# W_out issued second, w1 - w2 in quarters, w2 cast by GpSimd, and three first-stage matmuls in place of spins

## The chip, the cores and the metric

The kernel runs on one core of a Trainium2 chip. A core has TensorE (matrix products, into PSUM), VectorE (DVE in the profile), ScalarE (ACT), GpSimd (POOL) and SyncE (SP); each works through its own instructions in order, and waits on semaphores for the others. DMAs are issued from SyncE (the hardware queue, q1 in the profile) and from GpSimd (the software queue, q0, which also converts f32 to bf16 on the way). The metric is the device time of one execution in microseconds (us). Lower is better.

## The reference

The input x has 8 batches of 3072 rows and 256 columns, f32. Each column is filtered in the frequency domain, and the result goes through a gate of two weight matrices and an output matrix:

```python
X = np.fft.rfft(x, axis=1)
Y = X * (filt_r + 1j * filt_i)[None]
y = np.fft.irfft(Y, n=3072, axis=1).reshape(8 * 3072, 256)
h1, h2 = y @ w1, y @ w2                 # w1, w2: 256 x 1024
out = np.maximum(h1, h2) @ w_out        # w_out: 1024 x 256
```

## The kernel before

The gate is rewritten as max(h1, h2) = max(y (w1 - w2), 0) + h2. So out = relu(y Wd) W_out + y M, with Wd = w1 - w2 and M = w2 W_out, both made once on the chip. Wd comes from GpSimd (`prep_wd`, two halves of 512 columns). For M, VectorE casts w2 to bf16 (`cast_w2`, four casts of 512 columns), TensorE transposes it (`prep_t`, two halves), and 16 products with W_out follow (`prep_m`).

The Fourier transform of 3072 points is done in two stages of 96 and 32 as matmuls. For one batch: the first stage (`f1` for batch 1, `s1` for batches 2 to 7) over chunks of x; its result goes to a DRAM buffer `ad` and is read back in another layout as `bt`; the second stage (`s2`), the product with the filter on VectorE, and the inverse of the second stage (`s3`) follow; the result goes through a DRAM buffer `zd` and comes back as `zr`; the inverse of the first stage (`s4`) gives a tile `y` of 384 rows, transposed. Batch 0 avoids the DRAM buffers: it uses transposes on TensorE (`t1`, `t2`). For batches 2 to 7, x is loaded as f32 by SyncE (`load_xf`, eight chunks in three rotating buffers XF), and GpSimd adds and subtracts the two halves of the batch (`fold`, one add and one subtract a chunk); chunk c of `s1` needs fold c, and the load of chunk c + 3 needs fold c to have freed its buffer. For batches 0 and 1, x is loaded and cast by GpSimd's queue (`load_x`).

The main loop goes over 64 tiles `tt` of 384 rows plus one round to finish. Each tile has 8 steps. In a step, `moe_h` makes one block of 128 hidden units (two products with Wd, then a relu on ScalarE or VectorE into `gt`), and `moe_o` makes three or four of the 30 products of the tile before it (for each of three blocks c of 128 rows: eight with W_out and two with M, summed in PSUM tile `po`). Two neighbouring sums share a `po` tile, which VectorE copies to `ot`, and GpSimd's queue writes it to the output. Everything else hangs in this loop by step numbers: `plan(b, step, fn)` puts a function into step `step` of batch b's 64 steps, and all engines meet their instructions in this written order. `plan_f1` gives the steps of `f1` for batch 1 and of the read of `ad` (`f1_read`). `plan_f2` gives the visits of the next batch's second stage; in its first call they stand at steps 24, 28, 31, 35, 38, 42 and 46 of batch 0's 64, work on batch 1, and carry the `s1` chunks of batch 2 with them (chunk 0 at step 24, chunk 1 at step 28, chunk 2 at step 31). Its two last lists are the steps of `load_xf` and of `fold`.

Before the loop lies a setup: tables of sines, batch 0's first and second stage, the filter's products, and the loads of the weights. `spin` makes matmuls whose result nobody reads, while TensorE waits. At the end of the setup stand GpSimd's last loads of batch 1, the two halves of Wd, the load of W_out (`load_wo`), and the table CT that `s1` reads; then the first `f1`, `t2` and `s4`. Step 0 of the loop begins at about 37.5 us.

Tiles in the profile: Wo is W_out, WS holds w1 and w2 in f32, w2b and w2T are w2 cast and transposed, ph is a hidden block in PSUM, pa a first-stage result, px a second-stage result, pd a spin, xb is x in bf16.

Of the kernel before, what the change touches and what calls it, by code (L numbers as in the profile page):

```python
# [8 lines left out]
FP32 = mybir.dt.float32  # L9
# [6 lines left out]
D = 256  # L16
# [10 lines left out]
def kernel(  # L27
# [15 lines left out]
    V, S, G, TE = nc.vector, nc.scalar, nc.gpsimd, nc.tensor  # L43
# [15 lines left out]
    w2b = const.tile([128, 2, HID], BF16)  # L59
# [9 lines left out]
    pso = ctx.enter_context(tc.tile_pool(name="pso", bufs=2, space=bass.MemoryType.PSUM))  # L69
# [8 lines left out]
    def x_tile(b, c):  # L78
        if c % 2 == 0:
            xb[b] = xpool.tile([128, 8, D], BF16, tag="xb", name="xb")  # L80
        return xb[b][:, 4 * (c % 2):4 * (c % 2) + 4]

    def load_x(b, c, n):
        for k in range(c, c + n):
            xb[b, k] = x_tile(b, k)[0:NP]
        src = x[b].rearrange("(p m) d -> p m d", m=NM)
        m0 = 4 * (c % 2)
        G.dma_start(out=xb[b][0:NP, m0:m0 + 4 * n], in_=src[:, 4 * c:4 * c + 4 * n, :])  # L88
# [98 lines left out]
    def table_ct():  # L187
        G.memset(CT, 0.0)
        for g in range(2):
            G.tensor_copy(CT[64 * g:64 * g + 48, :, 0:48].rearrange("p s (u r) -> p s u r", r=2),  # L190
                          C1[0:48].rearrange("p (u s r) -> p s u r", s=2, r=2))
# [85 lines left out]
    w1f, w2f = WS[:, 0:2], WS[:, 2:4]  # L277
# [3 lines left out]
        nc.sync.dma_start(out=w1f[:, :, js], in_=moe_w1.rearrange("(c p) j -> p c j", p=128)[:, :, js])  # L281
        nc.sync.dma_start(out=w2f[:, :, js], in_=moe_w2.rearrange("(c p) j -> p c j", p=128)[:, :, js])

    def cast_w2(h, c):
        V.tensor_copy(w2b[:, c, 512 * h:512 * h + 512], w2f[:, c, 512 * h:512 * h + 512])

    def load_wo():
        G.dma_start(out=Wo, in_=moe_w_out.rearrange("(c p) j -> p c j", p=128))

    def prep_wd(h, engine):  # L290
        js = slice(512 * h, 512 * h + 512)
        engine.tensor_tensor(Wd[:, :, js], w1f[:, :, js], w2f[:, :, js], OP.subtract)  # L292

    def prep_t(jp):
# [22 lines left out]
    def f1(b, c, engine):  # L317
        if c == 0:
            ad[b] = dram.tile([96, NM, D], BF16, tag="ad", name="ad")
        if c % 4 == 0:  # L320
            at_[b] = apool.tile([128, 8, D], BF16, tag="at", name="at")
        at = at_[b]
        pa = ps.tile([96, 2, D], FP32, tag="ps", name="pa")
        TE.matmul(pa, C1, xb[b, c // 2][:, 2 * (c % 2):2 * (c % 2) + 2], start=True, stop=True)
        o_ = at[0:96, 2 * (c % 4):2 * (c % 4) + 2]
        if engine is V:
            V.tensor_copy(o_, pa)
        else:
            S.activation(o_, pa, AF.Copy)
        if c % 2 == 1:  # L330
            m0 = 2 * (c % 4) - 2
            nc.sync.dma_start(out=ad[b][:, 2 * c - 2:2 * c + 2], in_=at[0:96, m0:m0 + 4])
# [121 lines left out]
    po = {}  # L454
    ot = {}

    def out_block(tt, c):
        b, i = divmod(tt, 8)
        dst = out[b * N:(b + 1) * N].rearrange("(c p i m) d -> c i p (m d)", c=3, p=32, i=8)[c, i]
        E = G if tt < 8 * B - 2 else nc.sync  # L460
        E.dma_start(out=dst, in_=ot[tt // 2][:, 3 * (tt % 2) + c])  # L461

    def moe_o(tt, k0, k1):
        y_, g_ = yt[tt], gt[tt]
        for k in range(k0, k1):
            c, e = divmod(k, 10)
            n = (e + 2) % 10 if tt == 0 else e
            q = 3 * tt + c
            blk = slice(128 * c, 128 * c + 128)
            if e == 0 and (q % 2 == 0 or q == 24 * B - 1):  # L470
                po[0] = pso.tile([128, 2, D], FP32, tag="po", name="po")
            p_ = po[0][:, q % 2]
            if n < 2:
                TE.matmul(p_, y_[:, n, blk], M[:, n], start=(e == 0), stop=(e == 9))  # L474
            else:
                TE.matmul(p_, g_[:, n - 2, blk], Wo[:, n - 2], start=(e == 0), stop=(e == 9))  # L476
            if e == 9 and q >= 24 * B - 2:
                e = q % 6
                if q % 2 == 0:
                    S.activation(ot[tt // 2][:, e], p_, AF.Copy)  # L480
                else:
                    V.tensor_copy(ot[tt // 2][:, e], p_)
                out_block(tt, c)
            elif e == 9 and q % 2 == 1:
                if q % 6 == 1:
                    ot[tt // 2] = opool.tile([128, 6, D], FP32, tag="ot", name="ot")
                e = q % 6
                V.tensor_copy(ot[tt // 2][:, e - 1:e + 1], po[0])  # L488
                for qq in (q - 1, q):
                    out_block(qq // 3, qq % 3)  # L490

# [26 lines left out]
    def s3t(v, pq):  # L518
        pool, tag = (ps, "ps") if v % 2 else (pso, "po")
        pz = [pool.tile([128, 2, 2, 2, 2, NM], FP32, tag=tag, name="pt%d" % g) for g in range(2)]  # L520
        for _ in range(2 if v == 1 else 1):
            TE.matmul(pz[0].rearrange("p i s r c m -> p (i s r c m)"), W1[:, 0:128], W1, start=True, stop=True)
        for i in range(2):
            for s in range(2):
                for dc in range(2):
                    for q, tab in enumerate((VP, VQ)):
                        for g in range(2):
                            TE.matmul(pz[g][:, i, s, :, dc], pq[s][64 * g:64 * g + 64, q, i, 128 * dc:128 * dc + 128],  # L528
                                      tab[64 * g:64 * g + 64, 2 * v + i, s].rearrange("p (r m) -> p r m", r=2),
                                      start=(q == 0), stop=(q == 1))  # L530
        zv = zT.rearrange("p c m (w g) q -> p w g (c m) q", g=2)
        for g in range(2):
            o_ = zv[:, 2 * v:2 * v + 2, g]
            i_ = pz[g].rearrange("p i s r c m -> p i (c m) (s r)")
            if v >= 4 and g == 1:
                V.tensor_copy(o_, i_)
            else:
                S.activation(o_, i_, AF.Copy)

    def t2(c, engines):  # L540
        if c == 0:
            zr[0] = zrpool.tile([96, NM, D], BF16, tag="zr", name="zr")
        n = 4 // len(engines)
        for k, engine in enumerate(engines):
            pr = ps.tile([96, n, D], BF16, tag="ps", name="pr")
            m0 = 4 * c + n * k
            for m in range(n):
                for dc in range(2):
                    TE.transpose(pr[:, m, 128 * dc:128 * dc + 128], zT[:, dc, m0 + m].rearrange("p u q -> p (u q)"),  # L549
                                 I128)  # L550
            if engine is V:
                V.tensor_copy(zr[0][:, m0:m0 + n], pr)  # L552
            else:
                S.activation(zr[0][:, m0:m0 + n], pr, AF.Copy)

    def spin(n):
        for _ in range(n):
            pd = ps.tile([128, 512], FP32, tag="ps", name="pd")
            TE.matmul(pd, W1[:, 0:128], W1, start=True, stop=True)  # L559
# [70 lines left out]
        pqs[v] = products(v)  # L630
    for v in (4, 5):
        s3t(v, pqs[v])
    for c in (2, 4):
        load_x(1, c, 2)
    prep_wd(0, G)
    load_wo()
    load_x(1, 6, 2)
    prep_wd(1, G)
    table_ct()
    setup.close()  # L640
    apool = ctx.enter_context(tc.tile_pool(name="apool", bufs=3))
# [4 lines left out]
    f1(1, 0, S)  # L646
    spin(1)
    t2(0, (V, S))
    spin(2)
    s4(0)  # L650
    spin(2)


    todo = {}
# [1 line left out]
    def plan(b, step, fn, *a):  # L656
        todo.setdefault((b + step // 64, step % 64), []).append((fn, a))

    def plan_f1(b, nb, steps, read):
        for c, n in zip(range(1, 16), steps):  # L660
            plan(b, n, f1, nb, c, S if c % 2 == 0 else V)
        plan(b, read, f1_read, nb)

# [11 lines left out]
            plan(b, steps[-1] + (6 if b else 11), s1_read, b + 2)  # L675

    plan(0, 2, t2, 1, (V,))
    for h in range(2):
        for c in range(2):
            plan(0, 3 + 2 * h + c, cast_w2, h, c)  # L680
    plan(0, 5, prep_t, 0)
    plan(0, 7, prep_t, 1)
    plan(0, 8, prep_m)
    for c in range(2, 8):
        plan(0, 8 * (c - 2) + 8, t2, c, (V,))
    plan_f1(0, 1, (0, 1, 1, 3, 4, 4, 5, 6, 6, 7, 8, 10, 11, 11, 12), 13)
    plan_f2(0, (24, 28, 31, 35, 38, 42, 46), ((0,), (1,), (2,), (3,), (4,), (5,), (6, 7)),
            (6, 10, 14, 18, 21, 25, 29, 33), (14, 18, 21, 25, 28, 32, 36, 40))
    for b in range(1, B - 1):
        plan_f2(b, (7, 14, 18, 24, 31, 38, 42) if b > 1 else (14, 18, 24, 30, 34, 39, 42), ((0, 1), (2,), (3,), (4,), (5,), (6,), (7,)),  # L690
                range(-32, 32, 8) if b > 1 else range(-25, 31, 7), range(-22, 42, 8) if b > 1 else range(-15, 41, 7))
# [1 line left out]
    for tt in range(8 * B + 1):  # L693
        b, i = divmod(tt, 8)
        k = 0
        for j in range(8):
# [5 lines left out]
            if tt > 0:  # L702
                n = 3 if j in (3, 7) else 4
# [36 lines left out]
```

## Time and profile before

| what | value |
| --- | --- |
| runs | 504.0, 504.1 and 504.84 us, median 504.1 |
| profiled execution | 503.8 us, its span 502.0 us |
| TensorE busy | 488.4 us, 97% of the span |
| VectorE, ScalarE, GpSimd busy | 331.9, 308.3, 257.5 us |
| granted clock of TensorE, mean | 0.992 |
| W_out's load: issue, landing | 37.19, 9.4 us later |
| loads of batch 1's chunks 2 and 3, 4 and 5, 6 and 7: landing after issue | 5.3, 6.6 and 10.9 us, issued at 33.8, 34.4 and 38.1 |
| w1 - w2 on GpSimd | 2 x 2.36 us, at 34.90 and 38.65 |
| read of batch 1 (bt from ad) | two DMAs of 768 KB, issued from 56.88, landing 5.8 and 8.4 us after issue |

The span begins with the first instruction; all times of rows count from there. A row of the timeline has the start, the duration, the engine, the line, the operation, output and inputs, the shape, the count and, in brackets, the idle time of that engine just before it with the instruction or DMA that ended it (inferred: where that one had long been done, it was another). TensorE's rows overlap, as matmuls are pipelined: the time that a matmul takes from others is the distance of starts (0.109 us for one of 256 columns, 0.163 for 384, 0.217 for 512). Rows of SyncE (SPq) are the issue of DMAs. A row of the DMA queues has packets, MB, and the time that the packets took as a share of the 16 DMA engines.

### The profile page before, as it was taken

The page shows a single profiled execution, that of the slowest core. Times are in us where ns is not written, and L with a number is a line of the kernel's source. Part 1 is how long each engine was busy: PE and PEld are TensorE (multiplying, and loading weights), DVE is VectorE, ACT ScalarE, POOL GpSimd, SP SyncE. Part 2 cuts the span into 40 slices and gives each one's busy share as a digit, 9 for nine tenths or more (in the row PEclk, how much of TensorE's full clock was granted, in tenths as well). Part 3 has the DMA queues.
Part 4 walks back from the last instruction along what each step waited for, and adds up shares of the span by engine and source line. Part 5 has one row for each costly group of instructions (what it writes and reads, how often), then busy time and mean ns, then how long its engine had stood idle before and what let it go on. Part 6 is the DMA issues. An engine that isn't in the chain of part 4 may idle for free.

```text
span 502.0 us, 13079 instructions
## 1 busy us (share of the span) xinstructions
PE 488.4 (97%) x5299; PEld 362.1 (72%) x5303; DVE 331.9 (66%) x518; ACT 308.3 (61%) x629; POOL 257.5 (51%) x338
## 2 busy tenths in 40 slices
PE   8688999999999999999999999999999999999997
PEld 3455777777777777777777777777777777777775
DVE  7876688457865777457765687557765687555553
ACT  6776478647774676557764586647774465544442
POOL 7893569547463864645654855537632221222220
PEclk9989999999999999999999999999999999999999
DMA  7999789995799667986779558896769235411112
GB/s 125 150 252 217 230 229 290 306 274 171 212 268 260 175 204 234 250 229 189 198 244 275 187 177 245 235 239 197 197 181 255 78 111 153 168 65 64 64 64 84
DMA packets 77966, 97.20 MB, mean 194 GB/s; under 512 B 8017, under 2 KB 54354, under 8 KB 77842
## 3 DMA queue, kind: packets, MB, share of 16 engines
q1 hardware_dynamic: 64642, 66.73, 49.6%
q0 software_dynamic: 13264, 29.64, 20.3%
q8 instruction: 41, 0.67, 0.6%
q14 instruction: 19, 0.16, 0.1%
HBM read 53.87 MB, written 47.19 MB: 201 GB/s over the span
## 4 chain that ended last, share of the span: by engine, by line
PE 90%; DMA 5%; POOL 2%; issue 1%; ACT 1%; DVE 0%; SPq 0%; POOLq 0%; DVEq 0%
PE po L476 34%; PE ph L448 33%; PE po L474 8%; PE pz L399 5%; PE py L428 4%; PE pa L349 2%; DMA F<-in_filt_r_dram 2%; PE px L376 2%; DMA Wo<-in_moe_w_out_dram 2%; POOL xb L88 1%; DMA F<-F 1%; PE pr L549 1%; POOL pq L382 0%; PE pt L528 0%; PE pm__1132 L306 0%
## 5 line engine op out<-in xcount | busy, mean ns | idle before, releaser
L476 PE MATMUL po<-Wo,gt 128*128 128x256 bf16 x1536 | 261.0, 273 | 0.2 <-DMA Wo<-in_moe_w_out_dram 0.2
L452 ACT ACTIVATE gt<-ph 128x384 bf16<-128x384 f32 x321 | 157.0, 496 | 147.9 <-PE ph L448 147.3
L461 POOL DMA_DIRECT2D out_dram<-ot x186 | 102.6, 555 | 187.1 <-DVE ot L488 184.4
L476 PEld LDWEIGHTS <-gt 128*128 128x128 bf16 x1536 | 146.6, 98 | 66.1 <-issue 10.3
L450 DVE TENSOR_SCALAR gt<-ph 128x384 bf16<-128x384 f32 x191 | 104.9, 552 | 63.1 <-PE ph L448 59.9
L382 DVE TENSOR_TENSOR pq<-px,F 128x1024 bf16<-128x1024 f32 x91 | 107.0, 1219 | 24.2 <-PE px L376 22.6
L448 PEld LDWEIGHTS <-Wd 128*128 128x128 bf16 x1024 | 96.5, 98 | 12.9 <-POOL Wd L292 1.4
L103 POOL TENSOR_TENSOR xb<-XF 128x512 bf16<-128x512 f32 x48 | 61.2, 1276 | 41.3 <-DMA XF<-in_x_dram 21.2
L488 DVE COPY ot<-po 128x512 f32<-128x512 f32 x95 | 65.1, 685 | 25.3 <-PE po L476 25.0
L104 POOL TENSOR_TENSOR xb<-XF 128x512 bf16<-128x512 f32 x48 | 61.0, 1271 | 0.0
L403 ACT ACTIVATE zt<-pz 128x512 bf16<-128x512 f32 x84 | 45.6, 595 | 11.5 <-PE pz L399 8.4
L353 ACT ACTIVATE at<-pa 128x512 bf16<-128x512 f32 x96 | 51.8, 610 | 1.2 <-PE pa L349 0.8
L428 PE MATMUL py<-G,zr 96*128 96x96 bf16 x512 | 32.7, 206 | 0.2
L428 PEld LDWEIGHTS <-zr 96*128 96x128 bf16 x512 | 29.0, 97 | 2.5 <-DVE zr L552 0.4
L399 PE MATMUL pz<-pq,VP 64*64 64x256 bf16 x336 | 21.9, 281 | 0.0
L376 PE MATMUL px<-bt,U 64*64 64x256 bf16 x384 | 19.8, 278 | 1.2 <-ACT VQ L273 0.7
L399 PE MATMUL pz<-pq,VQ 64*64 64x256 bf16 x336 | 20.9, 269 | 0.0
L349 PE MATMUL pa<-xb,CT 64*64 64x512 bf16 x192 | 19.5, 383 | 0.0
L399 PEld LDWEIGHTS <-VP 64*64 64x64 bf16 x336 | 9.7, 105 | 13.3 <-issue 13.3
L376 PEld LDWEIGHTS <-U 64*64 64x64 bf16 x384 | 10.4, 109 | 3.9 <-issue 3.3
L559 PE MATMUL pd<-W 128*128 128x512 bf16 x30 | 10.5, 462 | 1.7 <-DVE zero L145 1.5
L552 DVE COPY zr<-pr 96x1024 bf16<-96x1024 bf16 (+1 forms) x8 | 5.2, 649 | 8.0 <-PE pr L549 8.0
(429 smaller groups left out, 609.7 us busy)
## 6 DMA issues: line engine op xcount, KB each, us to landing
out_dram<-ot POOLq DMA_DIRECT2D x186, 128.0 KB, 3.3
XF<-in_x_dram SPq DMA_DIRECT2D x96, 192.0 KB, 4.6
ad<-at SPq DMA_DIRECT2D x56, 192.0 KB, 3.3
bt<-ad SPq DMA_DIRECT2D x14, 768.0 KB, 9.1
zd<-zt SPq DMA_DIRECT2D x42, 256.0 KB, 2.7
zr<-zd SPq DMA_DIRECT2D x56, 192.0 KB, 4.8
WS<-in_moe_w_dram SPq DMA_DIRECT2D x4, 512.0 KB, 5.1
xb<-in_x_dram POOLq DMA_DIRECT2D x8, 192.0 KB, 5.8
```

The lines of the kernel that those rows point to most:

```text
L103: G.tensor_tensor(t_[:, 0], f[:, 0], f[:, 1], OP.add)
L104: G.tensor_tensor(t_[:, 1], f[:, 0], f[:, 1], OP.subtract)
L353: S.activation(at[:, m0:m0 + 2], pa[g], AF.Copy)
L382: E.tensor_tensor(pq, px.rearrange("p (o i) d -> p o i d", o=1).to_broadcast([128, 2, 2, D]), F[:, :, 2 * v:2 * v + 2, s], OP.mult)
L399: TE.matmul(pz[g][64 * s:64 * s + 64, i], tab[64 * g:64 * g + 64, 2 * v + i, s], pq[s][64 * g:64 * g + 64, q, i], start=(q == 0), stop=(q ...
L428: TE.matmul(py[:, m], zr[b][:, 4 * i + m, 128 * dc:128 * dc + 128], G1, start=True, stop=True)
L448: TE.matmul(ph, Wd[:, dc, 128 * j:128 * j + 128], y_[:, dc], start=(dc == 0), stop=(dc == 1))
L450: V.tensor_scalar(gt[tt][:, j], ph, 0.0, None, OP.max)
L452: S.activation(gt[tt][:, j], ph, AF.Relu)
L461: E.dma_start(out=dst, in_=ot[tt // 2][:, 3 * (tt % 2) + c])
L476: TE.matmul(p_, g_[:, n - 2, blk], Wo[:, n - 2], start=(e == 0), stop=(e == 9))
L488: V.tensor_copy(ot[tt // 2][:, e - 1:e + 1], po[0])
```

## The change

Four things are edited. W_out's load becomes the second of GpSimd's steps after the filter's products, behind one load of x; the two other loads of x go behind three quarters of w1 - w2. w1 - w2 is made in four parts of 256 columns. The cast of w2 goes from VectorE to GpSimd, in two parts, behind the last quarter. Three `f1` of batch 1 (c = 1, 2, 3) come before the loop, and three spins go. The step lists follow: the transposes of w2 stand at steps 7 and 8 (before 5 and 7), M at step 10 (before 8), the other `f1` at new steps, and the loads and folds of batch 2 at later steps (the read of `ad` stays at step 13, the visits where they were). The first tile's 30 output products come in a new order, `FIRST`: blocks 0 and 2 with W_out, then their four products with M, then block 1; two `po` tiles are open at once.

```diff
--- before.py
+++ after.py
@@ -281,14 +281,14 @@
         nc.sync.dma_start(out=w1f[:, :, js], in_=moe_w1.rearrange("(c p) j -> p c j", p=128)[:, :, js])
         nc.sync.dma_start(out=w2f[:, :, js], in_=moe_w2.rearrange("(c p) j -> p c j", p=128)[:, :, js])
 
-    def cast_w2(h, c):
-        V.tensor_copy(w2b[:, c, 512 * h:512 * h + 512], w2f[:, c, 512 * h:512 * h + 512])
+    def cast_w2(h):
+        G.tensor_copy(w2b[:, :, 512 * h:512 * h + 512], w2f[:, :, 512 * h:512 * h + 512])
 
     def load_wo():
         G.dma_start(out=Wo, in_=moe_w_out.rearrange("(c p) j -> p c j", p=128))
 
-    def prep_wd(h, engine):
-        js = slice(512 * h, 512 * h + 512)
+    def prep_wd(q, engine):
+        js = slice(256 * q, 256 * q + 256)
         engine.tensor_tensor(Wd[:, :, js], w1f[:, :, js], w2f[:, :, js], OP.subtract)
 
     def prep_t(jp):
@@ -460,16 +460,20 @@
         E = G if tt < 8 * B - 2 else nc.sync
         E.dma_start(out=dst, in_=ot[tt // 2][:, 3 * (tt % 2) + c])
 
+
+    FIRST = ([(c, e) for c in (0, 2) for e in range(8)] + [(c, e) for c in (0, 2) for e in (8, 9)]
+             + [(1, e) for e in range(10)])
+
     def moe_o(tt, k0, k1):
         y_, g_ = yt[tt], gt[tt]
         for k in range(k0, k1):
-            c, e = divmod(k, 10)
-            n = (e + 2) % 10 if tt == 0 else e
+            c, e = divmod(k, 10) if tt else FIRST[k]
+            n = e if tt else (e + 2) % 10
             q = 3 * tt + c
             blk = slice(128 * c, 128 * c + 128)
             if e == 0 and (q % 2 == 0 or q == 24 * B - 1):
-                po[0] = pso.tile([128, 2, D], FP32, tag="po", name="po")
-            p_ = po[0][:, q % 2]
+                po[q // 2 % 2] = pso.tile([128, 2, D], FP32, tag="po", name="po")
+            p_ = po[q // 2 % 2][:, q % 2]
             if n < 2:
                 TE.matmul(p_, y_[:, n, blk], M[:, n], start=(e == 0), stop=(e == 9))
             else:
@@ -485,7 +489,7 @@
                 if q % 6 == 1:
                     ot[tt // 2] = opool.tile([128, 6, D], FP32, tag="ot", name="ot")
                 e = q % 6
-                V.tensor_copy(ot[tt // 2][:, e - 1:e + 1], po[0])
+                V.tensor_copy(ot[tt // 2][:, e - 1:e + 1], po[q // 2 % 2])
                 for qq in (q - 1, q):
                     out_block(qq // 3, qq % 3)
 
@@ -630,12 +634,15 @@
         pqs[v] = products(v)
     for v in (4, 5):
         s3t(v, pqs[v])
-    for c in (2, 4):
+    load_x(1, 2, 2)
+    load_wo()
+    for q in range(3):
+        prep_wd(q, G)
+    for c in (4, 6):
         load_x(1, c, 2)
-    prep_wd(0, G)
-    load_wo()
-    load_x(1, 6, 2)
-    prep_wd(1, G)
+    prep_wd(3, G)
+    for h in range(2):
+        cast_w2(h)
     table_ct()
     setup.close()
     apool = ctx.enter_context(tc.tile_pool(name="apool", bufs=3))
@@ -646,9 +653,11 @@
     f1(1, 0, S)
     spin(1)
     t2(0, (V, S))
-    spin(2)
+    f1(1, 1, V)
+    spin(1)
     s4(0)
-    spin(2)
+    f1(1, 2, S)
+    f1(1, 3, V)
 
 
     todo = {}
@@ -657,7 +666,7 @@
         todo.setdefault((b + step // 64, step % 64), []).append((fn, a))
 
     def plan_f1(b, nb, steps, read):
-        for c, n in zip(range(1, 16), steps):
+        for c, n in zip(range(4, 16), steps):
             plan(b, n, f1, nb, c, S if c % 2 == 0 else V)
         plan(b, read, f1_read, nb)
 
@@ -675,17 +684,14 @@
             plan(b, steps[-1] + (6 if b else 11), s1_read, b + 2)
 
     plan(0, 2, t2, 1, (V,))
-    for h in range(2):
-        for c in range(2):
-            plan(0, 3 + 2 * h + c, cast_w2, h, c)
-    plan(0, 5, prep_t, 0)
-    plan(0, 7, prep_t, 1)
-    plan(0, 8, prep_m)
+    plan(0, 7, prep_t, 0)
+    plan(0, 8, prep_t, 1)
+    plan(0, 10, prep_m)
     for c in range(2, 8):
         plan(0, 8 * (c - 2) + 8, t2, c, (V,))
-    plan_f1(0, 1, (0, 1, 1, 3, 4, 4, 5, 6, 6, 7, 8, 10, 11, 11, 12), 13)
+    plan_f1(0, 1, (1, 2, 5, 6, 9, 9, 10, 10, 11, 11, 12, 12), 13)
     plan_f2(0, (24, 28, 31, 35, 38, 42, 46), ((0,), (1,), (2,), (3,), (4,), (5,), (6, 7)),
-            (6, 10, 14, 18, 21, 25, 29, 33), (14, 18, 21, 25, 28, 32, 36, 40))
+            (10, 14, 16, 18, 24, 27, 30, 33), (16, 21, 24, 26, 29, 32, 36, 40))
     for b in range(1, B - 1):
         plan_f2(b, (7, 14, 18, 24, 31, 38, 42) if b > 1 else (14, 18, 24, 30, 34, 39, 42), ((0, 1), (2,), (3,), (4,), (5,), (6,), (7,)),
                 range(-32, 32, 8) if b > 1 else range(-25, 31, 7), range(-22, 42, 8) if b > 1 else range(-15, 41, 7))
```

## The prediction

> **What bounds the kernel now.** I read the page's chain of work first: TensorE carries 90% of the span.
>
> ```profile
> PE 90%; DMA 5%; POOL 2%; issue 1%; ACT 1%; DVE 0%; SPq 0%; POOLq 0%; DVEq 0%
> ```
>
> Then the table of stretches, where the second and third numbers are the stretch's length and TensorE's busy time:
>
> ```profile
> 40.00:44.00 4.00, 3.31 (x30) 1.97 (x28) 3.90 (x10) 2.93 (x6) 1.82 (x4) 1.00 1.16 150
> 44.00:48.00 4.00, 3.12 (x28) 2.11 (x26) 1.89 (x4) 3.10 (x6) 0.00 (x0) 1.00 1.04 291
> 48.00:52.00 4.00, 4.00 (x38) 3.18 (x36) 1.75 (x3) 1.61 (x4) 0.00 (x0) 1.00 0.59 188
> 70.00:100.00 30.00, 30.00 (x359) 22.66 (x357) 21.91 (x32) 22.07 (x47) 23.61 (x28) 1.00 0.94 282
> ```
>
> TensorE never rests from 48 us to the last stretch, at a granted clock of 1.00. So a microsecond won before 48 us reaches the end only if nothing later makes TensorE wait, and a new wait is paid in full. Third, TensorE's timeline, for what it waits for before 48 us; the bracket is the idle time before the row:
>
> ```profile
> 41.07 0.50 PE L448 MATMUL ph<-y__984,Wd 128*128 128x384 bf16 x2 [0.67 <-POOL Wd L292]
> 45.35 0.56 PE L299 MATMUL pt<-I,w2b 128*128 128x128 bf16 x7 [0.70 <-DVE w2b L285]
> 46.64 0.60 PE L476 MATMUL po<-Wo,gt 128*128 128x256 bf16 x4 [0.18 <-DMA Wo<-in_moe_w_out_dram]
> ```
>
> These are the waits the edit touches: second half of w1 - w2, last cast of w2, W_out. The chain puts W_out last: GpSimd issues it at 37.19, and it lands 9.41 us later.
>
> Fourth, SyncE's queue and GpSimd's timeline around the first folds of batch 2:
>
> ```profile
> 56.88 1.22 SPq L338 DMA_DIRECT2D bt<-ad  x2
> 58.15 3.82 SPq L93 DMA_DIRECT2D XF<-in_x_dram  x1
> 62.01 0.47 SPq L97 DMA_DIRECT2D XF<-in_x_dram  x1
> 62.52 0.42 SPq L93 DMA_DIRECT2D XF<-in_x_dram  x1
> 62.99 0.43 SPq L97 DMA_DIRECT2D XF<-in_x_dram  x1
> ```
>
> ```profile
> 60.89 1.28 POOL L103 TENSOR_TENSOR xb<-XF 128x512 bf16<-128x512 f32 x1
> 62.11 1.28 POOL L104 TENSOR_TENSOR xb<-XF 128x512 bf16<-128x512 f32 x1
> 67.88 1.26 POOL L103 TENSOR_TENSOR xb<-XF 128x512 bf16<-128x512 f32 x1 [4.49 <-PE px L376]
> 69.11 1.26 POOL L104 TENSOR_TENSOR xb<-XF 128x512 bf16<-128x512 f32 x1
> ```
>
> The read of batch 1 (bt from ad) is issued at 56.88. The four DMAs of chunk 2 of batch 2 stand right behind it; the first is held 3.82 us at issue, and from 60 to 63 us the hardware queue is full (111.9%) with the read's small packets:
>
> ```profile
> q1 hardware_dynamic: 1979, 1.01, 111.9%
> ```
>
> By the landing times (8.3, 4.7, 4.9 and 4.7 us after issue) they arrive at 66.45, 66.71, 67.42 and 67.69, that is 10.8 us after the read's issue. The fold at 67.88 therefore waited for these loads; the name in its bracket (PE px) was long done. It cost nothing: its reader, the first-stage matmul of chunk 2, runs only at 71.86. Chunk 1 had been loaded by DMAs at 51.18 to 52.62, ahead of the read; its fold ended at 63.4, and its matmul came here:
>
> ```profile
> 67.63 0.39 PE L349 MATMUL pa<-xb,CT 64*64 64x512 bf16 x4
> ```
>
> **The change part by part.** The sum is made against the profiled execution, 503.8 us (span 502.0 and 1.8 around it), 0.3 below the median of the runs, 504.1. A change within 0.2% (1.0 us) can't be told from none here.
>
> *Three first-stage matmuls for three spins.* A f1 matmul and a spin have the same shape and take 0.217 us of TensorE each; they stand where TensorE waits for zr and y between 34.4 and 37.5, so nothing is lost there. VectorE's copy of f1 1 (0.68) fits between its zr copy (ends 36.19) and its y copy (37.17); those of f1 2 and 3 come behind the y copies, where both engines idle until 38.1. The first write of ad moves with them to about 37; SyncE has nothing else then. Gain: 3 x 0.217 = 0.65 us of work after 37.9.
>
> *GpSimd's queue.* The rows: a load of x 0.53, W_out 0.93, w1 - w2 on 128x1024 2.36, so a quarter (128x512) about 1.24, as the folds of that size show (1.26). New order: x chunks 2, 3 at 33.83; W_out 34.36 to 35.29; three quarters to 39.0; two loads of x to 40.0; last quarter to 41.3. The quarters are wanted (j = 0, 2, 4, 6) at 37.5, 39.4, 40.7 and 42.0, with work alone: none waits, and the 0.67 us goes. The load of chunks 2, 3 lands 5.3 after issue as before (39.1); f1 4 now comes at 38.3, so TensorE waits 0.9 there. That costs nothing as long as W_out ends last.
>
> *The casts.* VectorE loses 4 x 0.41 us, off the path. GpSimd's copy of 128x1024 from f32 isn't in the trace. Low bound: VectorE's two casts of half that size, 0.82. High bound: GpSimd's two-input row, 2.36. GpSimd's one-stream rows (IOTA 0.156 for 1 element, 0.262 for 128; MEMSET 0.106 and 0.213) grow by 0.83 ns an element, the two-input ones by about 2.1; a copy has one input, so I go by the former: 0.15 + 1024 x 0.00083 = 1.0. Casts end at 42.3 and 43.3, the CT table at 44.3 (read at 63, in cover). The transposes of w2 are reached at about 42.8 and, behind W_out, 44.7: no wait up to 1.5 us a cast. The Trainium skill, GPSIMD Engine Reference, section 4.1 (Engine selection), has one-input work at roughly the line rate and two-input work about 2x slower; the rows' 0.83 against 2.1 ns agree. By that page the cast stays under its limit of 1.5; by the two-input row it costs 1.3 us, which is a rival below.
>
> *W_out.* Before, two loads of x were ahead of it. The software queue began to move at 35; x packets went at 42 to 62 a us (96 packets a load, so about 2.1 us each), then the 1024 packets of W_out at about 250 a us. With one load fewer ahead: 46.6 - 2.1 = 44.5; the earlier issue alone would give 43.8 (34.36 + 9.41). I take 44.3. Ends: 43.1 (start 37.3, 4.1 of packets, 1.7 from the last packets, near 44.9 before, to the landing) and 46.6 (no gain). From its landing to the end of f1 15, TensorE has 19 W_out products (2.07), transposes of w2 and zT (0.44 + 0.45), four hidden blocks (1.30), eight f1 (1.74), M's matmuls (1.75): 7.75 us, so 52.05. Before, it was 46.64 + 6.66 = 53.30. Chunks 4, 5 of batch 1 stand right behind W_out in the queue and land 2.4 later, as the last load did (49.0 against 46.6): 46.7, wanted at 46.4. So 0.3 is given back; f1 15 ends at 52.36, 0.94 earlier. Chunks 6, 7 (49.1) are wanted at 51. M is read two steps after it is made; the second open sum takes the other PSUM buffer, whose next use is three steps later: nothing waits.
>
> *The XF loads.* Chunk 0 moves from step 6 to 10, chunk 1 from 10 to 14, their folds from 14 and 18 to 16 and 21. The read of batch 1 stays at step 13, so chunk 1's four DMAs now stand behind it on SyncE. The visit that reads chunk 1 stays at step 28. The read shifts with f1 15: 56.88 - 0.94 = 55.94. Chunk 1, in the place that chunk 2 had, lands 10.8 later, 66.74; the fold starts 0.2 later and takes 1.23 + 1.26: done at 69.43. TensorE stands at the matmul of chunk 1 at 67.63 - 0.94 = 66.69: a wait of 2.74 us. Ends of the landing: 9.2 (last issue 62.99 plus the 3.2 that such a load took at 52, against the read at 56.88) and 11.5 (output blocks 0 and 1, 256 KB, now reach their queue with the read; such a pair took 0.6 us at 63). I take 10.8, the row of the same position. Next: fold 2 is done 3.6 us after fold 1 (output issue 1.1, 2.5), its matmul comes 4.23 later (71.86 - 67.63): no second wait; folds 3 to 7 have more room. A z write that stands behind chunk 5's load is read ten steps later.
>
> Sum: -0.94 + 2.74 = +1.8 us: 505.6 against 503.8, so 505.9 on the scale of the median.
>
> **The rivals.**
> *Chunk 1 is there in time, faster.* If the loads landed within 8.1 us of the read, fold 1 would end before TensorE arrives, and the 0.94 stays: 503.2. That is its one condition. For it: loads in an idle queue land in 3.2 us. Against it: no load behind the read landed before +9.6 (66.45), and the second was only issued at +5.1. With W_out at 43.1 the gain would be 2.1.
> *Chunk 1 lands at its low end, no difference.* At +9.2 the wait is 1.1, the net +0.2: 504.3.
> *The cast costs 2.36.* The second ends at 46.0, the transposes wait 1.3 us; the wait for chunks 4, 5 goes (0.3). The first gain is gone, the wait for fold 1 stays: 506.9. Against it: the one-stream rows. W_out without a gain would give about the same or 0.7 more.
>
> **How the numbers follow.** Forecast as summed (505.2 to 506.6) 0.55; chunk 1 in time 0.21; chunk 1 at its low end 0.12; cast or W_out late 0.12. So slower 0.67, same 0.12, faster 0.21. The forecast is 505.9. The range goes from 503.2, the middle of the first rival, to 507.1, just over the last: about 0.15 is left out.
>
> **What would show it.** Right: a bracket of about 2.7 us before the chunk 1 matmul at L349 with TensorE idle for fold 1 (whatever name it bears); the fold's start 11 us behind the read; W_out's first product near 44.3; no bracket for Wd or w2b. Wrong: TensorE without a rest between 52 and 70 us (then the time is near 503); a cast row over 1.7 us; W_out landing after 46.

## The result, and the profile after

| kernel | median of its runs | lowest to highest | profiled execution | its span |
| --- | --- | --- | --- | --- |
| before | 504.05 us | 503.53 to 504.84 | 503.8 us | 502.0 us |
| changed | 508.74 us | 506.03 to 509.49 | 506.55 us | 504.8 us |

The changed kernel is slower, by a ratio of 1.008 (95% interval 1.0052 to 1.0107), 4.7 us between the medians. The direction and the place were forecast; the size was not: 505.9 was forecast, and 507.1 was the upper end. The profiled execution, at 506.55, is one of the changed kernel's quicker ones, which matters below.

TensorE's timeline of the changed kernel has no bracket left for Wd, w2b or W_out, and three new ones:

```profile
62.40 0.41 PE L376 MATMUL px<-bt,U 64*64 64x256 bf16 x8 [0.92 <-DMA bt<-ad]
...
69.43 0.37 PE L349 MATMUL pa<-xb,CT 64*64 64x512 bf16 x1 [2.13 <-POOL xb L103]
70.65 0.41 PE L349 MATMUL pa<-xb,CT 64*64 64x512 bf16 x3 [0.85 <-POOL xb L104]
```

The last two are the first-stage matmuls of chunk 1 of batch 2, which wait for the add and then for the subtract of its fold. The first is the second stage of batch 1, which waits for the read. GpSimd's timeline shows the fold, and ahead of it the casts of w2:

```profile
41.81 2.03 POOL L285 CAST w2b<-WS 128x1024 bf16<-128x1024 f32 x2
...
68.12 1.26 POOL L103 TENSOR_TENSOR xb<-XF 128x512 bf16<-128x512 f32 x1 [7.68 <-DMA XF<-in_x_dram]
69.34 1.26 POOL L104 TENSOR_TENSOR xb<-XF 128x512 bf16<-128x512 f32 x1
```

And SyncE's queue shows why the loads came so late: writes of ad, four DMAs of chunk 0, the last two writes of ad, the read, and only then chunk 1:

```profile
50.83 0.42 SPq L93 DMA_DIRECT2D XF<-in_x_dram  x1
51.30 0.44 SPq L97 DMA_DIRECT2D XF<-in_x_dram  x1
51.79 0.42 SPq L93 DMA_DIRECT2D XF<-in_x_dram  x1
52.26 0.43 SPq L97 DMA_DIRECT2D XF<-in_x_dram  x1
52.79 0.82 SPq L332 DMA_DIRECT2D ad<-at  x2
56.35 1.51 SPq L338 DMA_DIRECT2D bt<-ad  x2
57.91 3.20 SPq L93 DMA_DIRECT2D XF<-in_x_dram  x1
```

Step 0 of the loop (the first hidden block) began at 38.45 us, against 37.48 before. The delay is older than the edited instructions: VectorE's cast to zT in the setup began at 34.58 against 33.47, and the first instruction that an edit moves is GpSimd's load of W_out, at 34.92. Over the profiles of this case step 0 began anywhere from 37.48 to 38.75 us, the latest of them in a kernel with the front of before. So the two kernels are compared from step 0 on:

| from the start of step 0, us | before | changed | earlier (+) or later (-) |
| --- | --- | --- | --- |
| last f1 of batch 1 begins | 15.60 | 13.15 | +2.45 |
| read of batch 1 issued | 19.40 | 17.90 | +1.50 |
| second stage, visit at step 24 | 25.42 | 23.95 | +1.47 |
| first products behind chunk 1's matmul, step 28 | 30.46 | 32.54 | -2.08 |

The rows are starts less 37.48 and less 38.45; the changed kernel's last f1 is the second of a row of two that begins at 51.38. The front won 2.45 us, one microsecond of it was lost before the read, and the wait for chunk 1 took 3.55 more (the brackets of 2.13 and 0.85 leave out the matmul between them and the ends that the profile models). From there on TensorE is busy without a rest again. The profiled difference of the spans, 2.8 us, is the late start (0.97) and these 2.08, less 0.25 won later. That explains this execution, but not why the median lies 2.2 us above it.

### The profile page after: what moved, and what is told of

Its sections match the earlier page's. It is cut to its first block, busy times and chain, and to the rows that moved or that the text cites. A ratio compares the mean times of both kernels' runs of the same rounds, so it can differ in the third digit from the quotient of the medians.

```text
span 504.8 us, 13076 instructions
## 1 busy us (share of the span) xinstructions
PE 487.3 (97%) x5297; PEld 361.4 (72%) x5300; DVE 331.4 (66%) x514; ACT 308.5 (61%) x629; POOL 260.0 (52%) x342
## 4 chain that ended last, share of the span: by engine, by line
PE 86%; DMA 6%; POOL 4%; SPq 1%; issue 1%; DVE 0%; POOLq 0%
PE po L480 33%; PE ph L448 31%; PE po L478 8%; PE pz L399 5%; PE py L428 4%; PE pa L349 2%; PE px L376 2%; DMA F<-in_filt_r_dram 2%; DMA xb<-in_x_dram 1%; DMA XF<-in_x_dram 1%; POOL xb L88 1%; DMA F<-in_filt_i_dram 1%; POOL F L117 1%; DMA F<-F 1%; POOL Wd L292 1%
## 5 line engine op out<-in xcount | busy, mean ns | idle before, releaser
L349 PEld LDWEIGHTS <-CT 64*64 64x64 bf16 x192 | 8.8, 105 | 5.6 <-issue 3.4
L563 PE MATMUL pd<-W 128*128 128x512 bf16 x28 | 9.1, 435 | 1.5 <-DVE zero L145 1.5
```

## The experiments

Theory A: chunk 1 stands behind the read, and TensorE waits for it. Rival: the front itself (GpSimd's order, the casts) has become slower. The first four runs tell these apart.

**The changed kernel again** (no edit).

> The changed kernel as it is, to see how far its time and its waits between 52 and 72 us vary. Theory (chunk 1 of batch 2 is loaded behind the read of batch 1): 506 to 509.5 us, and TensorE idle for 2.5 us or more before the first-stage matmul of chunk 1 in its profile. Rival (the start of the kernel, before step 0, has become slower): the wait is 2 us or less and step 0 begins after 39 us when the time is above 508.

Measured: 509.61 us (507.12 to 512.74), ratio 1.0108 (1.0077 to 1.0139), just above the expected interval. Its profiled execution took 510.18 us, with the same two waits (2.43 and 0.68 in the brackets) and step 0 at 38.35. So the start does not explain the 3.6 us between the two profiles. The table of stretches explains the larger part; the columns behind the length are the busy times of TensorE, its weight loads, VectorE, ScalarE and GpSimd, then TensorE's granted clock and the DMA share:

```profile
70.00:71.00 1.00, 0.54 (x1) 0.10 (x1) 0.32 (x1) 0.00 (x0) 1.00 (x2) 0.72 0.98 176
71.00:72.00 1.00, 0.43 (x3) 0.13 (x2) 0.00 (x0) 0.00 (x0) 1.00 (x2) 0.50 0.18 37
...
74.00:75.00 1.00, 1.00 (x6) 0.64 (x5) 0.92 (x3) 0.02 (x1) 1.00 (x1) 0.50 0.88 264
...
77.00:78.00 1.00, 1.00 (x26) 0.66 (x27) 0.00 (x0) 0.49 (x1) 1.00 (x2) 0.87 0.33 70
78.00:79.00 1.00, 1.00 (x17) 0.61 (x10) 0.76 (x1) 0.98 (x3) 0.98 (x3) 1.00 0.99 313
```

In the first profile the clock stayed at 1.00 through the same stretch:

```profile
71.00:72.00 1.00, 1.00 (x17) 0.89 (x15) 0.02 (x1) 0.91 (x2) 0.98 (x3) 1.00 0.25 47
```

The first four W_out products behind the wait and the next inverse stage, by TensorE's timeline, here and then in the first profile:

```profile
72.14 1.04 PE L480 MATMUL po<-Wo,gt 128*128 128x256 bf16 x4
...
77.34 0.30 PE L399 MATMUL pz<-pq,VP 64*64 64x256 bf16 x4
```

```profile
70.99 0.61 PE L480 MATMUL po<-Wo,gt 128*128 128x256 bf16 x4
...
73.72 0.30 PE L399 MATMUL pz<-pq,VP 64*64 64x256 bf16 x4
```

Between these two rows the same instructions took 5.20 us against 2.73: 2.47 us more at the halved clock. Another 1.25 us of the 3.6 lie ahead of it: the first of these products came 33.79 us after step 0, against 32.54; an early f1 had waited 0.96 us for its load there, and the read was issued 0.8 us later after step 0. The halved clock became theory B: the wait can also let the granted clock fall, and what follows is then paid at half speed until it rises.

**The lists of before in the changed kernel.**

```diff
-            (10, 14, 16, 18, 24, 27, 30, 33), (16, 21, 24, 26, 29, 32, 36, 40))
+            (6, 10, 14, 18, 21, 25, 29, 33), (14, 18, 21, 25, 28, 32, 36, 40))
```

> The changed kernel with the loads and folds of batch 2 at the steps of the kernel before (6, 10, 14, ... and 14, 18, 21, ...). Theory: chunk 1 is loaded ahead of the read again, the wait before its matmul is gone, and the gain of the front is left: 1 to 2.5 us faster than before, 501.6 to 503.1 us. Rival (the front itself, GpSimd's new order and the casts, loses): 506 us or more.

Measured: 503.40 us (502.82 to 506.82) against 504.09, ratio 0.9998 (0.9983 to 1.0014); a second time 503.64 against 503.99, ratio 1.0 (0.9973 to 1.0026). The loss is gone, so the late lists cause it, as theory A has it, and the front has not become slower. But the expected gain was missed as well: the result can't be told from no change. The profiled execution (502.87) has two waits of its own, 0.59 us before the f1 of a later chunk and 0.42 before the second stage:

```profile
45.95 0.63 PE L324 MATMUL pa<-xb,C 96*96 96x512 bf16 x2 [0.59 <-DMA xb<-in_x_dram]
...
61.74 0.41 PE L376 MATMUL px<-bt,U 64*64 64x256 bf16 x8 [0.42 <-DMA bt<-ad]
```

**Only the late lists, in the kernel before.**

```diff
-            (6, 10, 14, 18, 21, 25, 29, 33), (14, 18, 21, 25, 28, 32, 36, 40))
+            (10, 14, 16, 18, 24, 27, 30, 33), (16, 21, 24, 26, 29, 32, 36, 40))
```

> The kernel before with only the loads and folds of batch 2 at the new steps (10, 14, 16, ... and 16, 21, 24, ...). Theory: the wait for fold 1 without the gain of the front: 2.7 us slower than before, 506.8 us (506 to 509). Rival: within 1 us of before.

Measured: 509.28 us (508.41 to 512.22), ratio 1.0112 (1.009 to 1.0133): 5.2 us slower, as much as the whole change, and above the expected interval, which priced the wait alone. The waits are those of theory A (2.12 and 0.85 in the brackets), and behind them the clock is at 0.50 from 73 to 76 us:

```profile
71.28 0.37 PE L349 MATMUL pa<-xb,CT 64*64 64x512 bf16 x1 [2.12 <-POOL xb L103]
72.50 0.61 PE L349 MATMUL pa<-xb,CT 64*64 64x512 bf16 x3 [0.85 <-POOL xb L104]
```

```profile
74.00:75.00 1.00, 1.00 (x11) 0.82 (x10) 0.24 (x1) 0.72 (x2) 1.00 (x2) 0.50 0.94 324
```

**Chunk 1 alone ahead of the read.**

```diff
-            (10, 14, 16, 18, 24, 27, 30, 33), (16, 21, 24, 26, 29, 32, 36, 40))
+            (10, 12, 16, 18, 24, 27, 30, 33), (16, 21, 24, 26, 29, 32, 36, 40))
```

> The changed kernel with one number changed: chunk 1 of batch 2 is loaded at step 12 in place of 14, so its four DMAs are issued ahead of the read of batch 1 at step 13. Theory: as with all lists put back, 501.6 to 503.6 us, no wait of over 0.5 us before the matmul of chunk 1. Rival (it is the amount of traffic with the read, not the place in the queue): the read lands later by what the four DMAs take (1.7 us) and TensorE waits for it instead, 505 to 507 us.

Measured: 505.53 us (503.97 to 508.53), ratio 1.0037 (1.002 to 1.0055). Both halves are partly right. The wait for chunk 1 is gone, but the read lands later (6.8 us after its issue for the first half, against 6.0 in the changed kernel, with the issue 17.90 us after step 0 in both), and TensorE waits for it:

```profile
62.84 0.41 PE L376 MATMUL px<-bt,U 64*64 64x256 bf16 x8 [1.67 <-DMA bt<-ad]
```

So both the place in the queue and the traffic around the read count. That a load which is through before the last writes of ad would be free is inferred from this; the kernel with both chunks at step 8, below, puts it to the test. The row is from the quickest execution of the twelve (503.97 us); the slower ones have no profile.

**Theory B on its own: spins in the wait.** If the clock falls because TensorE rests, then matmuls nobody reads should keep it up, at no other cost. In the visit of step 28:

```diff
         if n < 6:
             px = s2(b, n)
+        if (b, n) == (1, 1):
+            pd = ps.tile([128, 512], FP32, tag="ps", name="pd")
+            for _ in range(12):
+                TE.matmul(pd, W1[:, 0:128], W1, start=True, stop=True)
         if b + 1 < B:
```

In the kernel before with only the late lists:

> The kernel before with the late loads, and 12 spins of 512 columns (2.6 us of matmuls that nobody reads) between the second stage and the first-stage matmul of chunk 1 in the visit at step 28, where TensorE would wait. Theory (the wait itself costs about 2.7 us, and the granted clock that falls to a half behind it costs the rest of the 5.2 us): the clock stays at 1.00 from 70 to 80 us and the time is 506 to 507.5 us. Rival (the rest is lost in other waits, and the clock is only a sign of them): 508.5 to 510 us as without the spins.

Measured: 506.78 us (506.06 to 507.95), ratio 1.0063 (1.0041 to 1.0084). And in the changed kernel:

> The changed kernel with the same 12 spins in the same place. Theory (wait plus fall of the clock): 505 to 506.5 us, and the times lie within 2 us of each other. Rival: 508.5 us or more, spread over 3 us or more as without the spins.

Measured: 506.53 us (505.98 to 506.99), ratio 1.0052 (1.0033 to 1.007), a hair above the expected interval, and within 1.0 us of each other instead of 5.6. The rows of the first of the two, the spins and the clock behind them:

```profile
67.50 2.76 PE L417 MATMUL pd<-W 128*128 128x512 bf16 x12
70.19 0.59 PE L349 MATMUL pa<-xb,CT 64*64 64x512 bf16 x4
```

```profile
72.00:74.00 2.00, 2.00 (x32) 1.47 (x34) 1.32 (x3) 1.22 (x3) 2.00 (x3) 1.00 0.82 283
74.00:76.00 2.00, 2.00 (x34) 1.57 (x27) 1.66 (x2) 1.92 (x5) 2.00 (x2) 1.00 0.51 126
```

The same fold is waited for, and in the medians 2.5 us are won (509.28 to 506.78) by work that does nothing. Theory B holds: TensorE's rest is what lets the clock fall, and the fall costs time. How much is read from the stretch between the rows shown for the repeat: 2.73 us with the spins in both kernels, against 4.14 in the profile of the late lists and 5.20 in the repeat, so the clock costs 1.4 us in one execution and 2.5 in the other. The rest of the differences between these profiles lies ahead of that stretch. The spins did not shorten the wait in the changed kernel: from the second stage's matmul to the first W_out product it is 4.34 us with them, against 4.08 and 4.61 without. In the kernel before, where no front gains anything, the 2.8 us that remain with the spins are the price of the wait alone; the 2.5 of the changed kernel are net of what its front won.

Only profiles show when the clock fell, so how many executions it falls in is not known. All twelve runs of the changed kernel but one have a mean granted clock of 0.990 or less, and the three profiles with the late lists but no fall behind the wait have 0.993. But the mean also holds falls elsewhere (the profile of the late lists has one in its first 20 us), and 0.990 stands beside 506.03 as well as beside 509.08 us.

**W_out issued fourth again** (with the lists of before, to see what the front's gain is made of).

```diff
-    load_x(1, 2, 2)
+    for c in (2, 4):
+        load_x(1, c, 2)
+    for q in range(2):
+        prep_wd(q, G)
     load_wo()
-    for q in range(3):
+    load_x(1, 6, 2)
+    for q in range(2, 4):
         prep_wd(q, G)
-    for c in (4, 6):
-        load_x(1, c, 2)
-    prep_wd(3, G)
```

> The changed kernel with the lists of the kernel before, and W_out issued where it was before, behind two loads of x and half of w1 - w2 (the quarters, the casts on GpSimd and the three f1 stay). Theory (the gain of the front comes from W_out's earlier landing): W_out lands near 46.5 us and TensorE waits about 3 us for it, 504.5 to 506.5 us. Rival (the quarters and casts make the gain): 503 to 503.8 us as with W_out second.

Measured: 505.93 us (503.56 to 507.31), ratio 1.0033 (1.0014 to 1.0052), 2.5 us above the same kernel with W_out second. W_out landed at 45.9, and TensorE waited 2.34 us for it. Here too a wait of over 2 us is followed by a halved clock:

```profile
45.98 0.93 PE L480 MATMUL po<-Wo,gt 128*128 128x256 bf16 x4 [2.34 <-DMA Wo<-in_moe_w_out_dram]
```

```profile
47.00:48.00 1.00, 1.00 (x13) 1.00 (x11) 0.00 (x0) 0.20 (x1) 0.00 (x0) 0.50 0.98 275
```

So W_out's early issue is needed for a quick front; with the other parts alone the transposes and the hidden blocks are done sooner and TensorE stands before W_out longer than it did. Part of the 2.5 us is the halved clock's and not W_out's; the two were not separated here.

**Chunks 0 and 1 both at step 8**, so that SyncE has issued them before the last writes of ad are due:

```diff
-            (10, 14, 16, 18, 24, 27, 30, 33), (16, 21, 24, 26, 29, 32, 36, 40))
+            (8, 8, 14, 18, 21, 25, 29, 33), (14, 18, 21, 25, 28, 32, 36, 40))
```

> The changed kernel with the lists of the kernel before, but chunks 0 and 1 of batch 2 both loaded at step 8 (in place of 6 and 10), so that no load stands on SyncE between the last writes of ad. Theory (with the lists put back, the four issues of chunk 1 at 50.7 to 52.5 us hold the last two writes of ad back, and so the read): the read is issued by 55.3 us, no wait before the second stage at step 24, 501.5 to 503 us. Rival (the traffic moves into the loads of batch 1, and TensorE waits there instead): a wait of 0.8 us or more before the f1 of chunks 4 to 7, 503 to 505 us.

Measured: 503.03 us (501.55 to 505.23) against 504.00, ratio 0.9982 (0.9964 to 1.0), at the upper end of what was expected, with an interval that touches 1. SyncE's rows show the mechanism: the last three writes of ad go out together, and the read follows at 54.26, 16.7 us after step 0 (37.55) in place of 17.9:

```profile
49.91 2.38 SPq L332 DMA_DIRECT2D ad<-at  x3
54.26 1.18 SPq L338 DMA_DIRECT2D bt<-ad  x2
```

No wait is left before the second stage, and 0.32 us before an f1. It was run once more, beside the lists of before:

> Chunks 0 and 1 loaded at step 8, once more, since its interval touched 1. Theory (the read is issued a microsecond and more earlier against step 0, and no wait after it): 501.5 to 503.3 us in the median, the interval below 1. Rival (its first result was luck, it equals the kernel before): 503.5 to 504.3 us.

> The changed kernel with the lists of the kernel before, once more beside it on the same chip: 503 to 504 us. Theory: 0.4 us or more slower than chunks 0 and 1 at step 8, since the read is issued a microsecond later and TensorE waits for it at step 24. Rival: the same within 0.2 us.

Measured: 503.54 (501.27 to 507.34) and 503.64 us (502.45 to 507.58) against 503.99, ratios 0.9983 (0.9955 to 1.001) and 1.0 (0.9973 to 1.0026). So the rival of the first stands: no gain is proved. The profiled spans, 499.9 and 501.4, are in the order that was expected, but 1.06 of the 1.5 us is the start of step 0 (37.63 and 38.69); 0.4 is left from there on. The medians over the runs don't separate the two, and neither is proved faster than the kernel before. What makes their runs scatter over 5 to 6 us was not found, as none of the slower ones has a profile. With the lists of before, the three slowest of 23 (506.8 to 507.6 us) have the lowest mean granted clocks, 0.985 and 0.986, so there it goes with the clock; with both chunks at step 8 it does not (507.34 at 0.989, 501.50 at 0.989).

## Why the prediction was right in direction and wrong in size

**The wait for chunk 1: right in place, sized too small.** The loads behind the read were put at 10.8 us after it and the fold 0.2 later; the last load landed 11.5 after it and the fold began 11.8 after it. The wait was put at 2.74; by the starts it cost 3.55. The last landing took 5.7 us from its issue, against 4.7 for chunk 2 before, and TensorE arrived at the wait 0.5 us earlier after step 0 than forecast. The rival "chunk 1 is there in time" is excluded by the same rows.

**The step that failed: the price of a wait.** The prediction wrote that a new wait is "paid in full" and took TensorE's granted clock as 1.00 behind it. The runs show that a wait of that length can be paid about twice: 5.2 us for the late lists alone, of which 2.5 went away with the spins, and 2.47 us more for the same instructions in the repeat's profile, where the clock had fallen to 0.50. The trace of before showed such a fall, in its setup, which the prediction did not use: a thin stretch, then two stretches at half the clock. Every profile of this case has such a fall there; this is the one of before:

```profile
20.00:22.00 2.00, 1.16 (x54) 0.74 (x53) 1.97 (x2) 1.64 (x5) 2.00 (x2) 1.00 0.52 70
22.00:24.00 2.00, 0.62 (x32) 0.51 (x32) 1.50 (x3) 1.37 (x3) 1.95 (x3) 0.68 0.84 181
24.00:26.00 2.00, 1.70 (x57) 0.78 (x50) 2.00 (x2) 1.82 (x5) 1.98 (x1) 0.50 0.80 88
26.00:28.00 2.00, 1.64 (x42) 1.16 (x41) 2.00 (x3) 0.93 (x3) 2.00 (x2) 0.50 1.09 262
```

The Trainium skill, TensorE: Matmul & The Clock Gate, Part 1 (The HAM clock gate), says that the clock is granted at half or in full by how busy TensorE was in a window of about 3.4 us that runs freely, and its table under "Why this matters for your kernels" asks for no gap over some 3 us between bursts. The traces agree on half and full (0.50 and 1.00). On the length they are less lenient: brackets of 2.34 and of 2.43 us were enough in two profiles (in the repeat the clock averages 0.72 from 70 to 71 us, ahead of the second bracket), and of two nearly equal pairs one let it fall (2.12 and 0.85) and one did not (2.13 and 0.85). Equal waits with unequal ends are what a window that runs freely would give. That it is the window was not tested; that the rest is the cause was, by the spins.

**W_out and the front: right in sign in the profile, mis-sized.** W_out was put at 44.3, 6.8 us after step 0; it landed at 43.3, 4.9 after a later step 0, 8.4 us after its issue. The sum had the last f1 0.94 earlier; it was 2.45 earlier, and the wait of 0.3 for chunks 4 and 5 was not there in this profile. The wait before f1 4, put at 0.9, was missing here and 0.96 in the profile of the repeat. The early bound for the landing (43.1) was nearer than the value taken. From step 0 to the end of the span the profile of before took 464.5 us, and the two of the changed kernel with the lists of before took 463.2 and 462.7: there a gain of 1.3 to 1.8 us reaches the end. The medians don't prove it.

**The read: a term left out.** The prediction let the read move with the last f1. It moved by 1.50 where the f1 moved by 2.45. About half of the 0.95 us lost is SyncE's: the four issues of step 10 (chunk 0, 50.83 to 52.69) stand in front of the last two writes of ad, and the last write was issued 1.66 us after its f1, against 1.17 before. This is not the work of the moved lists: in the kernel before, chunk 1's issues stood in the same place (51.18 to 53.05), but the last f1 began only at 53.08 and so nothing was held. The other half lies between that write and the read (3.09 us against 2.63), and its cause stays open. The prediction counted what stands behind the read, and not what the writes stand behind. The visit at step 24 then waited 0.92 us. The kernel with chunks 0 and 1 at step 8 shows it from the other side: without those issues the last write is again 1.16 us behind its f1, the read is at 16.7 after step 0, and the wait is gone.

**The casts and quarters: right.** A cast took 1.05 us, 1.0 was worked out from GpSimd's one-stream rows; the two-input price of 2.36 did not come. The quarters took 1.28 each and no bracket names Wd. The Trainium skill's factor of two, which the prediction sets beside its rows for one and two inputs, compares GpSimd with VectorE; that comparison is 2.1 us against 1.21 for a product on 128x1024 in the changed kernel's profile, and 1.05 against two halves of 0.41 for the cast.

From step 0 on the profiled execution lost 2.08 us up to the first products behind the wait, near the forecast 1.8, but in part because two errors cancel: 1.47 won in place of 0.94, and 3.55 lost in place of 2.74. The median, 2.8 us over the forecast, needs the clock on top; how its 2.8 us divide between the clock and the starts of the single executions is not known.

## What to carry to other kernels

Before a new wait on TensorE is priced (here some 2.3 us were enough), look in the trace for a stretch where it rested and read the granted clock behind it: the work after the wait may run at half speed, and cheap matmuls in the gap can take that part away. When a transfer is moved in a queue, list what it now stands behind and also what it now stands in front of: here chunk 1 went behind a read whose halves land 6.0 and 8.7 us after its issue, and another load stood in front of the writes that the read waits for, which cost nothing until those writes came earlier. A time that is won before such a read counts only as far as the read itself is issued earlier: here 1.50 of 2.45 us.

## What the runs showed of the hardware that I had not expected

Equal waits of TensorE gave unequal ends: after 2.13 and 0.85 us of rest the clock stayed at 1.00, after 2.12 and 0.85 it went to 0.50 for some 3 us, after 2.43 and 0.68 for some 6 us; at 0.50 for most of it, a stretch that takes 2.73 us took 5.20. Twelve matmuls of 512 columns in the gap kept it at 1.00 in both kernels they were profiled in. The start of the loop moved between 37.48 and 38.75 us from profile to profile where the code ahead of it was the same.
